# Windowed attention and a top-1 mixture of experts: 32-row products in batches of four slices, a fourth place for raw weights, and a last pass of 160 columns

## The chip, the cores and the metric

The kernel runs on one core of a Trainium2 chip. A core has a matrix engine (TensorE, "PE" in the profile; its weight loads are listed as "PEld"), three engines for elementwise work (VectorE "DVE", ScalarE "ACT", GpSimd "POOL"), and a queue engine (SyncE "SP") that here issues most of the DMA transfers. The metric is the device time of one execution in microseconds; lower is better. Three runs of the kernel before took 619.26 to 623.4 us, with a median of 622.6 us.

## The reference

The input of the first part is q, k and v of 8 batches, 8 heads, 576 positions and 64 features. Each position attends to itself and the 63 positions before it. The result is laid out as a matrix `x` of 4608 rows and 512 columns, and that goes through a mixture of experts in which each row uses one expert only:

```
logits = x @ w_gate                     # 4608 x 8
expert = argmax(logits);  gate = softmax(logits)[expert]
for e in range(8):
    xe = x[expert == e]
    out[expert == e] = gate * (max(xe @ w1[e], 0) @ w2[e])     # 512 -> 1024 -> 512
```

Everything is 32-bit floating point. With these inputs the eight experts get 669, 400, 748, 505, 592, 390, 566 and 738 rows.

## The kernel before, in words

**Stages.** The first 165 us or so compute the attention in 36 tiles of 128 rows, write the rows of `x` to a buffer in device memory (`xs`) and rank them by expert as they come. From then on the expert work goes in *passes*. A pass takes one expert and up to four blocks of 128 of its rows, gathers the rows from `xs` by an indirect DMA on POOL, and runs over the 1024 hidden features in eight *slices* of 128. The four early passes (experts 0 to 3, 256 rows each) start while the rest is still being ranked. Eleven late passes follow; their number of columns (rows of `x`) is fixed when the program is built, and which expert each one takes is worked out on the chip.

**Precision.** TensorE has a fast form of 32-bit products, fp32r, which keeps fewer bits of each operand. The kernel splits each operand into a high part (`whi`, `xh`, `hh`) and a remainder (`wlo`, `xl`, `hl`) and makes three fp32r products of them. A slice of a pass of `w` columns is then: twelve products of `w` columns for the first layer (lines 340 and 344: four pieces of 128 input features times three), the ReLU and its split (ACT `hh` on line 352, DVE `hl` on line 356), and three products of 512 columns for each block of rows in the second layer (line 312). The splits of the weights are ACT `whi` (line 253) and DVE `wlo` (line 250), 1024 columns per slice. In `expert`, the second layer of slice j is issued after the first layer of slice j+1, through `late` and `flush`.

**A last block that is not full.** Where the last block of a pass has 32 or 64 rows, `few` returns that number. Its second layer then uses plain 32-bit products of the raw weights (line 308): the 32 rows (`hf`, 128 features by 32) fill a quarter of TensorE's columns, and four products of 128 output columns each stand side by side in the four quarters (for 64 rows, two products of 256). Each plain 32-bit product appears as two MATMUL records.

**Passes.** `SLOTS` lists what late passes there are beside those of 256 columns: two of 416, two of 512, one of 320, one of 384. `plan` gives experts to these by their number of blocks and by how many rows their last block lacks; its small operations (8 numbers each) run on POOL (helpers on lines 719, 721 and 726) and on DVE, and DVE waits for POOL between them. What is left over goes to passes of 256 columns, five of them with these inputs (`ALWAYS`); more would run behind conditions at the end. `ORDER` is the order of the eleven: 256, 320, 416, 416, 512, 512, 384, and four times 256.

**Raw weights.** An expert's weights come in four transfers of 1 MB, two slices each, into three places of the pool `wr` that are used in turn. SP issues them (line 235) in program order, together with the transposing DMAs that lay out gathered rows for the next pass (`DMA_TRANSPOSE`, line 868, three or four ahead of a wide pass) and the read of the next expert's number (line 269). `ready`, called after each slice, prepares the next pass: it opens its weights after slice 3 and loads more of them after slices 4 and 6; the fourth load comes while the pass runs, from `split_`. For a pass that follows one with raw 32-bit products the loads come later (`held`), since the raw weights must stay until those products are done. In the first late pass the three transposing DMAs of the pass of 320 columns stand on SP ahead of the fourth load.

The functions that the change touches are `Weights`, `few`, `flush`, `expert`, `plan`, `ready` and `open_weights`.

## Time and profile before

| | |
|---|---|
| runs, us | 619.26, 622.6, 623.4 (median 622.6) |
| profiled execution, us | 618.67 |
| its span, us | 616.9 |
| PE busy | 583.2 us (95% of the span) |
| DVE, ACT, POOL busy | 377.8, 358.6, 211.9 us |
| late passes, roughly | 264 us to 609 us |

How to read it: PE's records overlap, since matmuls are pipelined, so a busy share near 100% means that one product follows the other, and the cost of a product is read from the distance between two starts, not from its duration. The chain of waits is followed back from the last instruction. In a timeline row the first number is the start and the second the length in us; square brackets give the idle time of the engine ahead of it and who ended it.

### The profile page before, as it was taken

How to read it: one execution, taken by the hardware profiler on the slowest of the kernel's cores; microseconds unless marked ns; L12 is line 12 of the kernel's file. 1: busy time of each engine (PE TensorE's matmuls, PEld its weight loads, DVE VectorE, ACT ScalarE, POOL GpSimd, SP SyncE). 2: the span in 40 equal slices, each digit the busy share in tenths (PEclk: the TensorE clock that was granted, in tenths of full speed). 3: DMA queues.
4: the chain of work that ended last, by engine and by line, in shares of the span. 5: the costliest groups of instructions: out<-in, count | busy, mean ns of one | idle time of the engine just before them, and what ended most of it. 6: DMA issues, size and time to landing. Idle time of an engine off the chain costs nothing.

```text
span 616.9 us, 16023 instructions
## 1 busy us (share of the span) xinstructions
PE 583.2 (95%) x6555; PEld 497.1 (81%) x6555; DVE 377.8 (61%) x680; ACT 358.6 (58%) x759; POOL 211.9 (34%) x212
## 2 busy tenths in 40 slices
PE   8899898887999999998999999999999999999995
PEld 4688787776977888997778888788888899999994
DVE  4677678886676996656555554454444535667651
ACT  4577677676435665658654646436426446667752
POOL 3656657667447125041315051050120311132011
PEclk9999999999899999999999999999999999999998
DMA  8978888963586676895939367393292473886731
GB/s 301 379 252 295 278 256 293 304 204 111 190 306 204 241 250 178 305 244 199 230 113 302 122 181 232 137 258 126 82 265 91 116 265 104 295 272 203 266 132 35
DMA packets 71748, 132.85 MB, mean 215 GB/s; under 512 B 42604, under 2 KB 43756, under 8 KB 64240
## 3 DMA queue, kind: packets, MB, share of 16 engines
q1 hardware_dynamic: 65392, 112.84, 56.8%
q0 software_dynamic: 6272, 18.88, 9.3%
q8 instruction: 53, 0.87, 0.6%
q14 instruction: 31, 0.25, 0.1%
HBM read 104.44 MB, written 19.40 MB: 201 GB/s over the span
## 4 chain that ended last, share of the span: by engine, by line
PE 65%; issue 12%; POOL 9%; DVE 6%; DMA 4%; ACT 2%; SPq 0%; POOLq 0%; DVEq 0%; ACTq 0%
PE e_b L340 19%; PE e_b L312 12%; PE e_b L344 9%; PE x_b L312 5%; PE t_b L312 4%; POOL pm L486 4%; PE m_b L312 4%; PE x_b L500 3%; PE s_b L443 2%; PE m_b L517 2%; DMA ring<-qkv 2%; DVE wlo L250 1%; DMA raw<-wall 1%; POOL out L294 1%; DMA xs<-xrow 1%
## 5 line engine op out<-in xcount | busy, mean ns | idle before, releaser
L250 DVE TENSOR_TENSOR wlo<-raw,whi 128x1024 fp32r<-128x1024 f32 (+1 forms) x126 | 147.9, 1174 | 55.8 <-ACT whi L253 55.0
L352 ACT ACTIVATE hh<-e_b 128x256 fp32r<-128x256 f32 (+2 forms) x120 | 52.3, 436 | 176.5 <-PE e_b L344 175.8
L294 POOL DMA_INDIRECT out<-ys,idx_sb x32 | 44.2, 1382 | 261.3 <-ACT ys L291 255.8
L253 ACT CAST whi<-raw 128x1024 fp32r<-128x1024 f32 (+1 forms) x121 | 121.5, 1005 | 3.5 <-DMA raw<-wall 3.4
L340 PE MATMUL e_b<-xh,whi 128*128 128x256 f32 (+4 forms) x352 | 110.8, 331 | 2.2 <-ACT whi L253 2.2
L356 DVE SCALAR_TENSOR_TENSOR hl<-e_b,hh 128x256 fp32r<-128x256 f32 (+2 forms) x120 | 58.1, 484 | 86.9 <-ACT hh L352 65.0
L486 POOL TENSOR_TENSOR pm<-tsb,cs 128x512 f32<-128x512 f32 x72 | 90.2, 1273 | 52.4 <-ACT tsb L479 46.3
L340 PE MATMUL e_b<-xl,whi 128*128 128x256 f32 (+4 forms) x352 | 107.9, 323 | 0.0
L340 PEld LDWEIGHTS e_b<-xh,whi 128*128 128x128 f32 x352 | 66.3, 188 | 14.2 <-ACT whi L253 4.4
L344 PE MATMUL e_b<-xh,wlo 128*128 128x256 f32 (+4 forms) x352 | 70.6, 322 | 0.1
L340 PEld LDWEIGHTS e_b<-xl,whi 128*128 128x128 f32 x352 | 66.4, 189 | 4.7
L470 ACT ACTIVATE pf<-s_b,mxs 128x64 f32<-128x64 f32 x288 | 63.2, 337 | 9.7 <-DVE mxs L462 7.1
L500 PE MATMUL x_b<-ring,pm 64*64 64x65 f32 x2176 | 47.7, 224 | 13.1 <-issue 6.8
L344 PEld LDWEIGHTS e_b<-xh,wlo 128*128 128x128 f32 x352 | 56.4, 188 | 3.4 <-DVE wlo L250 0.5
L500 PEld LDWEIGHTS x_b<-ring,pm 64*64 64x64 f32 x2176 | 41.9, 135 | 19.2 <-issue 12.5
L312 PE MATMUL e_b<-whi,hl 128*128 128x512 f32 x144 | 56.4, 392 | 0.7 <-DVE hl L356 0.7
L312 PE MATMUL e_b<-wlo,hh 128*128 128x512 f32 x144 | 56.5, 392 | 0.0
L312 PE MATMUL e_b<-whi,hh 128*128 128x512 f32 x144 | 56.5, 392 | 0.0
L872 ACT COPY joined<-halves 128x1024 uint16<-128x1024 uint16 x36 | 47.8, 1352 | 0.0
L191 POOL DMA_INDIRECT rows<-xs,idx_sb x32 | 37.6, 1174 | 26.9 <-issue 26.0
L524 ACT COPY xT<-m_b 128x512 f32<-128x512 f32 x36 | 21.1, 587 | 42.4 <-PE m_b L517 42.3
L443 PE MATMUL s_b<-ring 64*64 64x128 f32 x1024 | 41.4, 277 | 1.1 <-DMA ring<-qkv 0.6
(203 smaller groups left out, 1005.7 us busy)
## 6 DMA issues: line engine op xcount, KB each, us to landing
raw<-wall SPq DMA_DIRECT2D x58, 1024.0 KB
ring<-qkv SPq DMA_DIRECT2D x66, 386.0 KB
xs<-xrow SPq DMA_DIRECT2D x36, 256.0 KB
raw<-wall SPq DMA_DIRECT2D x8, 256.0 KB
rows<-xs SPq DMA_DIRECT2D x2, 1024.0 KB
ring<-qkv SPq DMA_DIRECT2D x4, 256.0 KB
halves<-planes SPq DMA_TRANSPOSE x36
ring<-qkv SPq DMA_DIRECT2D x4, 130.0 KB
```

Source lines behind the costliest of these rows:

```text
L250: nc.vector.tensor_tensor(out=lo[:, s], in0=raw[:, s], in1=hi[:, s], op=ALU.subtract)
L253: nc.scalar.copy(out=hi[:, s], in_=raw[:, s])
L294: ins = nc.gpsimd.indirect_dma_start(out=out, out_offset=bass.IndirectOffsetOnAxis(ap=ix, axis=0), in_=ys[0:n], in_offset=None, bounds_che ...
L312: nc.tensor.matmul(y[0:n], lhsT=x[:, us], rhs=ww[:, C:], start=(j == 0 and m == 0), stop=(j == NJ - 1 and m == 2))
L340: nc.tensor.matmul(hp[:, 0:w], lhsT=hi[:, ks], rhs=x[:, kk, 0:w], start=(kk == 0 and x is xh), stop=False)
L344: nc.tensor.matmul(hp[:, 0:w], lhsT=lo[:, kk * P:(kk + 1) * P], rhs=xh[:, kk, 0:w], start=False, stop=(kk == 3))
L352: nc.scalar.activation(out=hh[:, 0:r], in_=hp[:, 0:r], func=AF.Relu)
L356: nc.vector.scalar_tensor_tensor(out=hl[:, 0:r], in0=hp[:, 0:r], scalar=0.0, in1=hh[:, 0:r], op0=ALU.max, op1=ALU.subtract)
L443: nc.tensor.matmul(sp[cols, a, g], lhsT=q_r[rows, r, g], rhs=k_r[rows, r - 1:r + 1, g], start=True, stop=True)
L470: nc.scalar.activation(out=pf[:, g, a], in_=sp[:, a, g, 0], func=AF.Exp, bias=mx[:, h:h + 1], scale=SCALE)
L486: nc.gpsimd.tensor_tensor(out=pm[i], in0=t.rearrange("p (g q) -> p g q", g=NG), op=ALU.mult, in1=cc("mask")[:, i * P:(i + 1) * P].unsqueez ...
L500: nc.tensor.matmul(x_b[cols, a, g * V1:(g + 1) * V1], lhsT=pm[i][rows, g, cols], rhs=v_r[rows, c % RING - i, g], start=(i == 0), stop=(i = ...
```

## The change

The 64-row case of raw products goes away: `few` is true for 32 rows only, so the pass of 320 columns makes its last block with three fp32r products like any other. The 32-row products are collected over four slices (`some`, `BATCH`) and issued together, sixteen products in a row. The raw weights of slices 0 to 3 of such a pass must stay until then, so there is a fourth place for raw weights: `place`, which is the memory of two of the early passes' buffers of gathered rows (`xg[1]` and `xg[2]`, now one tile `xgs`). In late passes the second of the four transfers goes there, and the last load is issued after slice 0 of the running pass.

There is a new kind of pass, one of 160 columns: a full block and 32 rows. `plan` has a row for it (`p4`, `c4`), and one pass of 256 columns less is always there (`ALWAYS` 4). It is the last in `ORDER`. The experts 1 and 2 change places (`PERM`), on the host for the weights and the gate, so the four early passes still take the first four. The expert of 400 rows then needs two late blocks, the second with 16 rows, and it fits the new pass; four passes of 256 columns remain. Spacers (`SPACE`) and widths of small tables follow.

```diff
-SLOTS = ((4, 416, 2), (4, 512, 2), (3, 320, 1), (3, 384, 1))
+SLOTS = ((4, 416, 2), (4, 512, 2), (3, 320, 1), (3, 384, 1), (2, 160, 1))
+KINDS = len(SLOTS) + 1
+PERM = (0, 2, 1, 3, 4, 5, 6, 7)
...
-ALWAYS = 5
-TAIL = [5, 6, 8, 12, 18]
-ORDER = (6, 4, 0, 1, 2, 3, 5, 7, 8, 9, 10)
+ALWAYS = 4
+TAIL = [4, 5, 7, 11, 17]
+ORDER = (7, 4, 0, 1, 2, 3, 5, 8, 9, 10, 6)
...
+BATCH = 4
...
-    xg = [const.tile([P, 2, C], F32, name=f"xg{i}") for i in range(3)]
+    xgs = const.tile([P, 3, 2, C], F32, name="xgs")
+    xg = [xgs[:, i] for i in range(3)]
+    place = xgs[:, 1:3].rearrange("p i u c -> p i (u c)")
...
-            raw = self.raws[jj] = wr.tile([P, 2, 2 * C], F32, name="raw")
+            raw = place if self.late and jj == 1 else wr.tile([P, 2, 2 * C], F32, name="raw")
+            self.raws[jj] = raw
...
-            if self.far and not self.held and r and self.loaded < min(jj + 3, NJ // 2):
+            if self.far and r and self.loaded < min(jj + 3, NJ // 2):
                 self.load()
...
     def few(w):
 
-        n = w % P
-        return n if n in (LQ, W) else 0
+        return w % P == LQ
...
             if hf is not None and u + 1 == len(yp):
-                k = P // n
-                for g in range(k):
-                    nc.tensor.matmul(y[g * n:(g + 1) * n, 0:C // k], lhsT=hf[:, 0:n],
-                                     rhs=raw[:, C + g * C // k:C + (g + 1) * C // k], start=(j == 0), stop=(j == NJ - 1))
+                some.append((j, hf, raw))
+                if len(some) == BATCH:
+                    for i, x, ww in some:
+                        for g in range(QUAD):
+                            nc.tensor.matmul(y[g * LQ:(g + 1) * LQ, 0:P], lhsT=x, rhs=ww[:, C + g * P:C + (g + 1) * P],
+                                             start=(i == 0), stop=(i == NJ - 1))
+                    some.clear()
...
-            n = few(w)
-            r = w - n
+            r, hf = w, None
+            if few(w):
+                r, i = w - LQ, j % BATCH
+                hfs = hw.tile([P, BATCH, LQ], F32, name="hfs", bufs=2) if i == 0 else hfs
+                hf = hfs[:, i]
...
-            if wts.held and j % 2 == 0 and wts.loaded < j // 2 + 3:
+            if wts.late and j in (0, 2):
                 wts.load()
...
-        ev = of("ev2", two("ev", half, 2.0, ALU.is_ge), two("even", odd, 0.5, ALU.is_lt), ALU.mult)
-        of("ev3", ev, two("few", spare, float(P - LQ), ALU.is_ge), ALU.mult, want2[:, 0])
+        ev = of("ev2", two("even", odd, 0.5, ALU.is_lt), two("few", spare, float(P - LQ), ALU.is_ge), ALU.mult)
+        of("ev3", ev, two("ev", half, 2.0, ALU.is_ge), ALU.mult, want2[:, 0])
+        pair = of("pair", ev, two("one2", half, 1.0, ALU.is_ge), ALU.mult)
...
-        p3 = of("p3", odds, cm[:, 2], ALU.subtract)
+        of("p3", odds, cm[:, 2], ALU.subtract, more2[:, 0])
+        of("p4", pair, cm[:, 0], ALU.subtract, more2[:, 1])
...
         l1 = of("l3", two("third", cm[:, 3], -3.0, ALU.mult), l1, ALU.add)
+        l1 = of("l3b", two("pairs", cm[:, 4], -2.0, ALU.mult), l1, ALU.add)
...
-        wts[i] = Weights(expert_of(passes[i][0]), far=True, held=few(widths[i]) > 0)
+        wts[i] = Weights(expert_of(passes[i][0]), late=True)
...
+    order = list(PERM)
+    moe_w1, moe_w2, moe_w_gate = moe_w1[order], moe_w2[order], moe_w_gate[:, order]
```

Three places where the program's instructions move. The first is on PE, between two slices of a pass of 416 columns (`m_b`, `t_b` and the `e_b` of the second layer are accumulators of the four blocks; `xh` and `xl` belong to the first layer of the next slice). Before, each slice has this:

```order
L312 MATMUL t_b<-whi,hh 128x512
L312 MATMUL t_b<-wlo,hh 128x512
L312 MATMUL t_b<-whi,hl 128x512
L308 MATMUL m_b<-raw,hf 32x128 x4
L340 MATMUL e_b_3376<-xh,whi 128x416
L340 MATMUL e_b_3376<-xl,whi 128x416
```

Now, after the fourth slice and after the eighth, and nothing of the kind after the others:

```order
L324 MATMUL t_b<-whi,hh 128x512
L324 MATMUL t_b<-wlo,hh 128x512
L324 MATMUL t_b<-whi,hl 128x512
L319 MATMUL m_b<-raw,hfs 32x128 x8
L319 MATMUL m_b<-xgs,hfs 32x128 x8
L352 MATMUL e_b_3375<-xh,whi 128x416
L352 MATMUL e_b_3375<-xl,whi 128x416
```

Four groups of four products became one group of sixteen, half of it from the fourth place (`xgs`).

The second is on SP, from the third weight load of the first late pass on. Before:

```order
L235 DMA raw<-wall 128x2048
L868 DMA_TRANSPOSE halves<-planes 128x8x128 x3
L235 ISA
L235 DMA raw<-wall 128x2048
L269 TENSOR_LOAD es_sb
```

Now:

```order
L242 DMA raw<-wall 128x2048
L242 ISA
L242 DMA raw<-wall 128x2048
L888 DMA_TRANSPOSE halves<-planes 128x8x128 x3
L276 TENSOR_LOAD es_sb
```

The fourth load moved from behind the three transposing DMAs to ahead of them.

The third is on POOL, in `plan` (`want` is what DVE waits for next). Before:

```order
L719 TENSOR_SCALAR ev<-halfr 128x8
L719 TENSOR_SCALAR even<-odd 128x8
L726 TENSOR_TENSOR ev_3891<-ev,even 128x8
L719 TENSOR_SCALAR few<-spare 128x8
L726 TENSOR_TENSOR want_3842<-ev_3891,few 128x8
L719 TENSOR_SCALAR less<-spare 128x8
L726 TENSOR_TENSOR want_3842<-odds,less 128x8
L726 TENSOR_TENSOR p_3957<-odds,cm 128x8
```

Now:

```order
L733 TENSOR_SCALAR even<-odd 128x8
L733 TENSOR_SCALAR few<-spare 128x8
L740 TENSOR_TENSOR ev_3890<-even,few 128x8
L733 TENSOR_SCALAR ev<-halfr 128x8
L740 TENSOR_TENSOR want_3841<-ev_3890,ev 128x8
L733 TENSOR_SCALAR one_3895<-halfr 128x8
L740 TENSOR_TENSOR pair<-ev_3890,one_3895 128x8
L733 TENSOR_SCALAR less<-spare 128x8
L740 TENSOR_TENSOR want_3841<-odds,less 128x8
L740 TENSOR_TENSOR more_3960<-odds,cm 128x8
L740 TENSOR_TENSOR more_3960<-pair,cm 128x8
```

Two operations more stand ahead of the second `want`, one more right after it, and two (`pairs`, `l3b`) further down.

## Rows read from the trace of the kernel before

**Rows 1.** Page, parts 2 and 4: PE by slices of 15.4 us; the chain.
```profile
PE   8899898887999999998999999999999999999995
...
PE 65%; issue 12%; POOL 9%; DVE 6%; DMA 4%; ACT 2%; SPq 0%; POOLq 0%; DVEq 0%; ACTq 0%
```

**Rows 2.** Timeline of PE, one slice of the first pass of 416 columns.
```profile
325.96 0.39 PE L312 MATMUL t_b<-whi,hl 128*128 128x512 f32 x1
326.28 0.43 PE L308 MATMUL m_b<-raw,hf 128*32 128x128 f32 x8
326.64 0.46 PE L340 MATMUL e_b<-xh,whi 128*128 128x416 f32 x1
326.94 0.35 PE L340 MATMUL e_b<-xl,whi 128*128 128x416 f32 x1
327.13 0.35 PE L340 MATMUL e_b<-xh,whi 128*128 128x416 f32 x1
```

**Rows 3.** Timeline of PE in the attention stage: gate products and what follows.
```profile
64.81 1.08 PE L561 MATMUL m_b<-xT,wg_sb 128*32 128x128 f32 x32 [0.24 <-ACT xT L524]
65.83 1.10 PE L443 MATMUL s_b<-ring 64*64 64x128 f32 x32
```

**Rows 4.** Timeline of PE, one slice of the pass of 320 columns.
```profile
304.69 0.39 PE L312 MATMUL m_b<-whi,hl 128*128 128x512 f32 x1
305.00 0.65 PE L308 MATMUL x_b<-raw,hf 128*64 128x256 f32 x4
305.59 0.42 PE L340 MATMUL e_b<-xh,whi 128*128 128x320 f32 x1
```

**Rows 5.** Timeline of PE's weight loads, behind the raw products of rows 2.
```profile
326.64 0.19 PEld L340 LDWEIGHTS e_b<-xh,whi 128*128 128x128 f32 x1 [0.20 <-issue]
326.75 0.19 PEld L340 LDWEIGHTS e_b<-xl,whi 128*128 128x128 f32 x1
```

**Rows 6.** Timeline, the last slice of the last pass (256 columns) and the end.
```profile
605.07 0.28 PE L340 MATMUL e_b<-xh,whi 128*128 128x256 f32 x1
605.19 0.28 PE L340 MATMUL e_b<-xl,whi 128*128 128x256 f32 x1
...
606.50 0.39 PE L312 MATMUL e_b<-whi,hh 128*128 128x512 f32 x1
...
607.19 0.39 PE L312 MATMUL e_b<-whi,hh 128*128 128x512 f32 x1
...
608.75 1.37 ACT L291 ACTIVATE ys<-e_b,gate_sb 128x512 f32<-128x512 f32 x2 [1.67 <-PE e_b L312]
...
610.99 0.98 POOL L294 DMA_INDIRECT out<-ys,idx_sb  x1 [0.30 <-DVEq L1106]
```

**Rows 7.** Timeline of SP, ACT and PE in the first late pass.
```profile
264.10 5.85 SPq L868 DMA_TRANSPOSE halves<-planes  x3
...
278.40 1.04 ACT L253 CAST whi<-raw 128x1024 fp32r<-128x1024 f32 x1 [2.71 <-DMA raw<-wall]
...
279.50 0.39 PE L340 MATMUL e_b<-xh,whi 128*128 128x256 f32 x1 [1.43 <-ACT whi L253]
...
283.65 0.39 PE L340 MATMUL e_b<-xh,whi 128*128 128x256 f32 x1 [0.80 <-ACT whi L253]
```

**Rows 8.** Chain of waits in the same pass: the fourth load.
```profile
270.20 8.18 DMA raw<-wall
```

**Rows 9.** Timeline of POOL in `plan`.
```profile
191.20 0.23 POOL L719 TENSOR_SCALAR less<-spare 128x8 f32<-128x8 f32 x1
191.51 0.20 POOL L726 TENSOR_TENSOR want<-odds,less 128x8 f32<-128x8 f32 x1
...
193.88 1.07 POOL L726 TENSOR_TENSOR l<-four,left 128x8 f32<-128x8 f32 x1
```

**Rows 10.** Waits, 190 to 290 us: engine, for whom, us, times, longest.
```profile
DVE c02r L736 <- POOL want L726: 3.7, 1, 3.7
...
PE x_b L312 <- DVE hl L356: 1.1, 1, 1.1
```

More of the change, by code (lines that the diff above doesn't have):

```diff
@@ L72 @@
 AHEAD = 2
-SPACE = (159, 232)
+SPACE = (135, 48)
 SPLIT = 26
@@ L84 @@
                ("st0", E), ("eid", E), ("tcol", NT), ("row", P), ("first", 2 * EARLY), ("pcol", 1), ("scol", 1), ("ucol", 1),
-               ("kind", 5), ("at", 5)):
+               ("kind", KINDS), ("at", 5)):
     CO[_n] = (_off, _w)
@@ L105, in constants @@
     put("mask", np.concatenate([p % W <= q, p % W > q], 1))
-    put("desc", E - e)
+    put("desc", E - np.array(PERM)[None])
     put("ebase", REG * P * e)
@@ L122, in constants @@
     put("ucol", ucol[:, None])
-    is_ = kind[:, None] == np.arange(5)[None]
+    is_ = kind[:, None] == np.arange(KINDS)[None]
     put("kind", is_)
-    last = is_[:, 0] | is_[:, 2]
-    put("at", np.stack([last, -4 * is_[:, 0] - 3 * is_[:, 2], ~last, 3 * (is_[:, 1] | is_[:, 4]), 4 * is_[:, 4]], 1))
+    last = is_[:, 0] | is_[:, 2] | is_[:, 4]
+    put("at", np.stack([last, -4 * is_[:, 0] - 3 * is_[:, 2] - 2 * is_[:, 4], ~last, 3 * (is_[:, 1] | is_[:, 5]),
+                        4 * is_[:, 5]], 1))
     return c
@@ L178, in window_attention_then_top1_moe @@
     ones = const.tile([P, P], BF16, name="ones")
-    starts = const.tile([P, 5 * E], F32, name="starts")
+    starts = const.tile([P, KINDS * E], F32, name="starts")
     ones_f = const.tile([P, P], F32, name="ones_f")
@@ L209, in window_attention_then_top1_moe, with __init__ @@
     class Weights:
-        def __init__(self, ev, spread=0, far=False, held=False):
-            self.far, self.held = far, held
+        def __init__(self, ev, spread=0, far=False, late=False):
+            self.far, self.late = far, late
             self.ev, self.loaded, self.given, self.raws = ev, 0, 0, {}
@@ L269, in expert_of @@
         return nc.sync.value_load(es_sb[m:m + 1, 0:1], min_val=0, max_val=E - 1)
-    late = []
+    late, some = [], []
     def few(w):
-        n = w % P
-        return n if n in (LQ, W) else 0
+        return w % P == LQ
     def flush(final=False):
@@ L286, in finish @@
             ys = hw.tile([P, C], F32, name="ys", bufs=5)
-            k = P // n if hf is not None and u + 1 == len(yp) else 1
-            for g in range(k):
-                o, i = ys[0:n, g * C // k:(g + 1) * C // k], yp[u][g * n:(g + 1) * n, 0:C // k]
-                if g == 0:
-                    nc.scalar.activation(out=o, in_=i, func=AF.Copy, scale=gate)
-                else:
-                    nc.vector.tensor_scalar(out=o, in0=i, scalar1=gate, scalar2=None, op0=ALU.mult)
+            if hf is not None and u + 1 == len(yp):
+                for g in range(QUAD):
+                    o, i = ys[0:n, g * P:(g + 1) * P], yp[u][g * LQ:(g + 1) * LQ, 0:P]
+                    if g == 0:
+                        nc.scalar.activation(out=o, in_=i, func=AF.Copy, scale=gate)
+                    else:
+                        nc.vector.tensor_scalar(out=o, in0=i, scalar1=gate, scalar2=None, op0=ALU.mult)
+            else:
+                nc.scalar.activation(out=ys[0:n], in_=yp[u][0:n], func=AF.Copy, scale=gate)
             ins = nc.gpsimd.indirect_dma_start(
@@ L408, in window_attention_then_top1_moe @@
     nc.vector.memset(starts, 1.0)
-    for k in range(5):
+    for k in range(KINDS):
         nc.vector.memset(starts[:, k * E:k * E + 1], 0.0)
@@ L767, in plan @@
             yield
-        stt("c3", running("c3r", p3)[:, 0], float(SLOTS[3][2]), p3, ALU.is_le, ALU.mult, out=cm[:, 3])
+        ends = running("c34r", more2.rearrange("p k e -> p (k e)"), 2)
+        stt("c3", ends[:, 0], float(SLOTS[3][2]), more2[:, 0], ALU.is_le, ALU.mult, out=cm[:, 3])
+        stt("c4", ends[:, 1], float(SLOTS[4][2]), more2[:, 1], ALU.is_le, ALU.mult, out=cm[:, 4])
         yield
         l1 = of("l3", two("third", cm[:, 3], -3.0, ALU.mult), l1, ALU.add)
+        l1 = of("l3b", two("pairs", cm[:, 4], -2.0, ALU.mult), l1, ALU.add)
         p1 = two("p1", l1, 4.0, ALU.is_ge)
@@ L776, in plan @@
         l1 = of("l4", two("fourth", cm[:, 1], -4.0, ALU.mult), l1, ALU.add)
-        floor_of("ns", two("l5", l1, 0.0, ALU.max), 0.5, 0.25, cm[:, 4])
+        floor_of("ns", two("l5", l1, 0.0, ALU.max), 0.5, 0.25, cm[:, KINDS - 1])
         for _ in range(WAIT[3]):
             yield
-        sums = running("sums", cm.rearrange("p k e -> p (k e)"), 5)
-        nc.vector.tensor_copy(out=tot_sb, in_=sums[:, 4, E - 1:E])
+        sums = running("sums", cm.rearrange("p k e -> p (k e)"), KINDS)
+        nc.vector.tensor_copy(out=tot_sb, in_=sums[:, KINDS - 1, E - 1:E])
         yield
@@ L784, in plan @@
         kind, at = cc("kind"), cc("at")
-        mine = rt.tile([P, 5, E], F32, name="sums_", bufs=1)
-        nc.vector.tensor_tensor(out=mine, in0=sums, in1=kind.unsqueeze(2).to_broadcast([P, 5, E]), op=ALU.mult)
+        mine = rt.tile([P, KINDS, E], F32, name="sums_", bufs=1)
+        nc.vector.tensor_tensor(out=mine, in0=sums, in1=kind.unsqueeze(2).to_broadcast([P, KINDS, E]), op=ALU.mult)
         ends = small("ends")
@@ L899, in ready @@
         prepare(j, late_rows[i % 2], len(passes[i]), i, columns_of)
-        held = i > 0 and few(widths[i - 1]) > 0
+        held = i > 0 and few(widths[i - 1])
         if j == 3 + held:
```

10 lines of the change are left out of this document (5 added, 5 removed).

## The prediction, made before the changed kernel was run

> **What bounds the kernel now.** I read the page first. From the second half of the span on, PE's slices show 9 throughout, and of the chain that ended last 65% is PE [rows 1]. So in the late passes the time is the sum of PE's steps, and a step is the distance between the starts of two products. Then I read the timeline of PE for one slice of each kind of pass that the change touches [rows 2, 4, 6], to get these steps; then the places where PE had to wait: the first late pass, where a weight load came late [rows 7, 8], and the stretch around 190 us, where DVE waits for the small operations of `plan` on POOL and PE waits for DVE [rows 10].
>
> **32-row products in batches.** In a pass of 416 columns the last fast product of a slice is followed after 0.32 us, where its step is 0.23 [606.50 to 607.19 for three, rows 6]: 0.09 more. The raw products take 0.36 to the start of the next kind, and the first product of that kind takes 0.30 where the next takes 0.19: 0.11 more [rows 2]. Together 0.56 us per slice, 16 slices in the two passes: 9.0 us. The attention stage has exactly the new pattern: the gate's products, 32 records of 128 columns with 32 weight columns each, side by side in four quarters. From their start to the next kind it is 1.02 us [rows 3]. A batch then costs 0.09 + 1.02 + 0.11 = 1.22 us, and there are four: 4.9. The gain is **4.1 us**. If the batch did not overlap its four groups, it would take 4 x 0.36 + 0.20 = 1.64, and the gain would be 2.4; I take the row of the same pattern.
>
> **The pass of 320 columns.** Its raw products cost 0.31 - 0.23 = 0.08, then 0.59 [rows 4], then 0.11 as in rows 2: 0.78 us per slice. Three fast products of 512 columns take 0.69 [rows 6]. Over eight slices that is a gain of **0.7 us**. No fast product with 64 weight columns is in the trace; if changing to that width and back costs what it costs the raw ones, 0.19 per slice, it is a loss of 0.8. I take the gain, since the stream of columns is that of rows 6. `hh` and `hl` get a quarter longer there; ACT and DVE wait for PE in these passes, so this costs nothing as long as PE is the bound.
>
> **The last pass.** It has 160 columns where it had 256, and its second block makes raw products. The first layer has 12 products per slice with a step of 0.12 [605.07 to 605.19, rows 6]. What a step of 160 columns takes, no row shows. The steps at 512, 416 and 256 columns are 0.23, 0.19 and 0.12 [rows 2, 6], a line that gives 0.08 at 160. But each product has a weight load of 128 columns of its own, and where two loads stand back to back with nothing before them, the second starts 0.11 after the first [rows 5]. A step cannot then be shorter than the load, and I take 0.11: 8 x 12 x 0.01 = 1.0 us gained. The ends are 0.12 (nothing) and 0.08 (3.8 us).
> The Trainium skill says of weight loads the same (TensorE: Matmul & The Clock Gate, LDWEIGHTS): their time goes with the stationary operand's columns, about 107 ns for 128, whatever streams afterwards. This speaks against narrowing the pass, and by it the first layer would give next to nothing; the trace agrees, with its 0.11. The same page's section on the back-to-back gap gives an isolated product of 160 columns 69 ns, and the first layer would then give 4.9 us.
> The second layer loses the second block's three products. The end hangs on the moment when the first block of the last slice is done, at 608.75 [rows 6], so seven of the eight count: 7 x 0.69 = 4.8. Of the two batches the first counts, 1.22. The second runs after 608.75, and it has 2.24 us until the second scatter would start on POOL at 610.99 [rows 6], which it does not reach: free. Its cover is POOL's first scatter; without that, 1.2 us. Together this pass gives 1.0 + 4.8 - 1.2 = **4.6 us** (3.6 to 7.4).
>
> **The fourth place and the order of loads.** In the first late pass the three transposing DMAs hold SP from 264.10 for 5.85 us [rows 7], the fourth load starts at 270.20 and takes 8.18 us [rows 8], ACT waits 2.71 us for it, and PE loses 1.43 and, as ACT is then behind, 0.80 [rows 7]. In the new program this load stands ahead of the transposing DMAs, and the buffer that it takes was last read in the early pass before. Issued at 264.10 at the latest, even with 8.18 it lands at 272.3, ahead of 275.7, when ACT first asked (278.40 - 2.71). I take the whole 2.23: **2.2 us**. The ends are 0 (other transfers fill the room) and 2.7. What SP then issues behind it, the transposing DMAs, is asked for much later. In the other passes loads come a slice or two earlier than before, and PE waited for none; no gain.
>
> **The plan.** POOL gets five small operations more. One takes 0.23 or 0.20 and the next starts 0.31 later [rows 9], but 1.07 can also happen (193.88, while DVE ran a wide operation). Two stand ahead of `want`, for which DVE waits 3.7 us while `hl` is queued behind that wait and PE waits 1.1 us for `hl` [rows 10]: 0.6 us straight onto PE. The other three come ahead of later waits of the same chain, where PE's products still cover something; I count two thirds of their 0.9. Together **1.2 us lost** (0.5 to 2.5, if two of them take 1.07).
>
> The early passes read other experts' weights and rows, in the same numbers; DVE's scans of 48 instead of 40 numbers are below what can be told. These cost nothing.
>
> **Sum.** -4.1 - 0.7 - 4.6 - 2.2 + 1.2 = **-10.4 us**. The profiled execution took 618.67, so it would take 608.3. That one is faster than all three runs shown, whose median of 622.6 lies 3.9 above it; for the median of runs I say **612.2 us**. The bounds together, not all at one end, make 608.5 to 616.
>
> **Rivals.**
> *The fast product falls back below 256 columns.* Every fast product in the trace streams 256 columns or more; should a narrower one run like a plain 32-bit product, the last pass would be slower. A round of four plain ones, side by side, adds (1.02 - 0.36) / 3 = 0.22 us per 128 columns [rows 2, 3], 0.28 for 160. Then 96 products cost 96 x (0.28 - 0.12) = 15.4 more instead of 1.0 less, and the sum is +6.0: 628.6 us. It decides from a step of 0.22 on: (10.4 - 1.0) / 96 over 0.12. For it speaks only that nothing narrower was ever used here; against it, that the steps from 512 down to 256 lie on a line. 7%.
> *The columns alone decide.* Weight loads hide, the step is 0.08, the sum -13.2: 609.4 us. For it: at 256 columns loads and products overlap without a gap [rows 6]. Against it: 0.11 between two loads [rows 5]. This is what the gap formula quoted above would give. 13%.
> *The stall is moved, not removed, and the plan costs its worst.* The fourth load now shares its time with the transposing DMAs, and the loads of the next pass with the gathers; an 8.18 us landing [rows 8] shows how crowded it is. Then 2.2 is not gained and 1.3 more is lost: -6.9, 615.7 us. 16%.
> *The plan does not do what it says*, and a fifth pass of 256 columns runs behind the conditions: eight slices of 0.12 x 12 + 0.69 x 2 = 2.82 us [rows 6], 22.6 more: 634.8 us. The rows per expert speak against it: 400 rows are two early blocks and two late ones, the last with 16 rows. 2%.
> The forecast itself: 57%. 5% stay for what I have not seen.
>
> **The numbers.** The range takes in the forecast's own bounds, the second and third rival, and a microsecond or two for the spread of the runs, which is 4 us: 607.5 to 618. It leaves out the two slower cases, the unseen, and tails, about 2 in 10. A change under 1% (6.2 us) can't be told from none here; that is 616.4. Faster by more: nearly all of the forecast and of the second case, over half of the third, 0.77. Within 1%: 0.13. Slower: 0.10.
>
> **What would show it.** In the profile after, each pass of 416 columns has two groups of 32 records of about 1.0 us, and slices without one are 0.56 us shorter; the last pass has a step of 0.11 and a slice of about 2.0 us instead of 2.8; PE's two gaps in the first late pass are gone, and ACT's wait for the load with them; the gap of 1.1 around 191 us has grown to some 1.7. A step of 0.2 or more in the last pass, a DMA as the releaser of ACT's `whi`, or PE's busy share falling in the late passes would make it wrong.

## The result and the profile after

The changed kernel takes **610.41 us** (median; 610.16, 610.67, 609.82, 616.26) where the kernel before, its three runs shown ahead and one more of 618.6, takes 620.93. The ratio of the fast runs is 0.9858, 95% interval 0.981 to 0.9907 (that of the two medians is 0.983), so it is faster, by 1.4% or a little more. The forecast was 612.2 us and a change of -10.4. The profiled execution takes 610.16 us (span 608.4) against 618.67 (616.9): -8.5.

Two profiled executions can be compared only from the early passes on. Up to there the kernels of the ten runs below are nearly the same program, and yet the slice that starts at 159.74 us in the changed kernel's trace starts at 155.9 to 162.5 in theirs. From there on the granted clock is 1.00 both before and after (ahead of it 0.98 and 1.00), so the clock does not enter into the differences. The table goes by the starts of slices (the first product of a first layer), each stretch by its own length.

| stretch (us, before; after) | before | after | difference | forecast |
|---|---|---|---|---|
| start to a slice of the early passes (159.50; 159.74) | 159.50 | 159.74 | +0.2 | 0 |
| `plan` (to 211.78; 213.01) | 52.28 | 53.27 | +1.0 | +1.2 |
| rest of the early passes (to 261.00; 262.50) | 49.22 | 49.49 | +0.3 | 0 |
| first late pass (to 286.87; 285.76) | 25.87 | 23.26 | -2.6 | -2.2 |
| pass of 320, its last second layer included (to 321.78; 320.02) | 34.91 | 34.26 | -0.65 | -0.7 |
| passes of 416, likewise (to 400.37; 394.59) | 78.59 | 74.57 | -4.0 | -4.1 |
| 512, 384 and three of 256 (to 585.47; 579.70) | 185.10 | 185.11 | 0.0 | 0 |
| last pass to its first result copy (608.75; 599.07) | 23.28 | 19.37 | -3.9 | } |
| from there to the start of the last scatter (610.99; 602.64) | 2.24 | 3.57 | +1.3 | } -4.6 |
| end | 5.89 | 5.73 | -0.2 | 0 |

Four of the five terms of the forecast's sum hold to 0.4 us. The fifth, the last pass, gives 2.6 instead of 4.6.

The page answers to [rows 1]: PE by 40 slices, and the shares of the chain. PE stays the bound.
```profile
PE   8788889798898999999999999999999999999994
...
PE 74%; POOL 9%; DVE 6%; issue 6%; DMA 3%; ACT 2%; SPq 0%; POOLq 0%; DVEq 0%; ACTq 0%
```

The timeline of PE where a batch stands in a pass of 416 columns, and the next slice's start, answer to [rows 2]:
```profile
337.07 0.39 PE L324 MATMUL t_b<-whi,hl 128*128 128x512 f32 x1
337.39 0.64 PE L319 MATMUL m_b<-raw,hfs 128*32 128x128 f32 x16
337.85 0.62 PE L319 MATMUL m_b<-xgs,hfs 128*32 128x128 f32 x16
338.40 0.46 PE L352 MATMUL e_b<-xh,whi 128*128 128x416 f32 x1
338.69 0.35 PE L352 MATMUL e_b<-xl,whi 128*128 128x416 f32 x1
```
The batch is 32 records as in [rows 3], 16 from each of two buffers of weights (`xgs` is the new place): 0.32 from the last fast product, where its step is 0.23, then 1.01, then 0.29 where the next step takes 0.19 as in [rows 2]. That is 0.09 + 1.01 + 0.10 = 1.20 (forecast 1.22). Slices without a batch take 4.32 us, before 4.88.

The pass of 320 columns, beside [rows 4]: the third block's products now step at 0.23, like every other, with 64 weight columns and without a price at either end.
```profile
303.76 0.39 PE L324 MATMUL x_b<-wlo,hh 128*64 128x512 f32 x1
303.99 0.39 PE L324 MATMUL x_b<-whi,hl 128*64 128x512 f32 x1
304.21 0.31 PE L352 MATMUL e_b<-xh,whi 128*128 128x320 f32 x1
```

SP's queue and PE in the first late pass, beside [rows 7, 8]: the weight loads stand ahead of the transposing DMAs, and PE's two gaps of 1.43 and 0.80 have become one of 0.19. The two slices behind the late load, which took 4.39 and 4.15 us, take 2.80 and 3.15.
```profile
252.44 8.42 SPq L242 DMA_DIRECT2D raw<-wall  x2
265.60 5.65 SPq L888 DMA_TRANSPOSE halves<-planes  x3
...
282.56 0.38 PE L352 MATMUL e_b<-xh,whi 128*128 128x256 f32 x1 [0.19 <-ACT whi L260]
```

`plan`, beside [rows 9, 10]: DVE's wait for `want` and PE's for DVE now, then DVE's next wait in `plan`, before and now (engine, for whom; us, times, longest).
```profile
DVE c02r L750 <- POOL want L740: 4.1, 1, 4.1
...
PE x_b L324 <- DVE hl L370: 1.6, 1, 1.6
...
DVE c1r L736 <- POOL p L719: 1.8, 1, 1.8
...
DVE c1r L750 <- POOL p L733: 2.3, 1, 2.3
```
PE's wait for `hl` grew from 1.1 to 1.6, as the prediction had it for the two operations ahead of `want` (forecast 1.7). Two further stalls, 0.2 and 0.3 us in the slices at 206 and 209, come behind DVE's wait for `p`, which grew by 0.5: `pairs` and `l3b` stand ahead of it on POOL. DVE's own operations there, one of them new and some wider, took only hundredths more each.

The last pass, beside [rows 6]: a first layer, the start of its second layer, and the next slice.
```profile
594.12 0.23 PE L352 MATMUL e_b<-xh,whi 128*128 128x160 f32 x1
594.19 0.28 PE L352 MATMUL e_b<-xl,whi 128*128 128x160 f32 x1
594.30 0.28 PE L352 MATMUL e_b<-xh,whi 128*128 128x160 f32 x1
...
595.42 0.43 PE L324 MATMUL e_b<-whi,hh 128*128 128x512 f32 x1
595.68 0.39 PE L324 MATMUL e_b<-wlo,hh 128*128 128x512 f32 x1
...
596.15 0.24 PE L352 MATMUL e_b<-xh,whi 128*128 128x160 f32 x1
```
The step at 160 columns is 0.11, as forecast; the twelve products take 1.30 (594.12 to 595.42), before 1.43. The three of the second layer take 0.73 instead of 0.69, since the first step behind the narrow products is 0.26. The slice takes 2.03, 0.04 more than forecast.

And the end, PE, ACT, DVE and POOL in order of time:
```profile
598.97 1.08 PE L319 MATMUL e_b<-raw,hfs 128*32 128x128 f32 x32
599.07 0.69 ACT L302 ACTIVATE ys<-e_b,gate_sb 128x512 f32<-128x512 f32 x1 [1.06 <-PE e_b L324]
600.03 0.97 POOL L303 DMA_INDIRECT out<-ys,idx_sb  x1 [14.88 <-ACT ys L302]
600.12 0.36 ACT L298 ACTIVATE ys<-e_b,gate_sb 32x128 f32<-32x128 f32 x1 [0.35 <-PE e_b L319]
600.50 1.07 DVE L300 TENSOR_SCALAR ys<-e_b,gate_sb 32x128 f32<-32x128 f32 x3 [2.17 <-ACT ys L298]
602.64 0.88 POOL L303 DMA_INDIRECT out<-ys,idx_sb  x1 [1.63 <-issue]
```
Here is the loss. POOL's first scatter is over at 601.0, the second starts only at 602.64. Ahead of it stand, one behind the other: the batch (to 600.1), one copy on ACT, three on DVE that wait for ACT's (to 601.57), and 1.07 in which POOL waits for nothing that the profile shows.

A second, smaller loss is in the third slice of this pass, which takes 2.35 instead of 2.03. ACT makes two result copies of the pass before (581.93 and 582.63) ahead of `whi`; DVE's `wlo` follows late, and PE's next products begin at 585.56, 0.35 behind the one before:
```profile
582.63 0.69 ACT L302 ACTIVATE ys<-x_b,gate_sb 128x512 f32<-128x512 f32 x1
583.21 1.04 ACT L260 CAST whi<-xgs 128x1024 fp32r<-128x1024 f32 x1
...
584.28 1.22 DVE L257 TENSOR_TENSOR wlo<-xgs,whi 128x1024 fp32r<-128x1024 f32 x1 [2.39 <-ACT whi L260]
...
585.21 0.27 PE L352 MATMUL e_b<-xl,whi 128*128 128x160 f32 x1
585.56 0.68 PE L356 MATMUL e_b<-xh,wlo 128*128 128x160 f32 x4
```

### The profile page after: what moved, and what is told of

Same layout as the page of the kernel before. It is cut to its first block, busy times and chain, and to the rows that moved or that the text cites. A ratio compares the mean times of both kernels' runs of the same rounds, so it can differ in the third digit from the quotient of the medians.

```text
span 608.4 us, 16098 instructions
## 1 busy us (share of the span) xinstructions
PE 571.4 (94%) x6587; PEld 494.4 (81%) x6587; DVE 379.3 (62%) x684; ACT 357.3 (59%) x759; POOL 210.6 (35%) x217
## 3 DMA queue, kind: packets, MB, share of 16 engines
q0 software_dynamic: 6224, 18.88, 10.4%
## 4 chain that ended last, share of the span: by engine, by line
PE 74%; POOL 9%; DVE 6%; issue 6%; DMA 3%; ACT 2%; SPq 0%; POOLq 0%; DVEq 0%; ACTq 0%
PE e_b L352 21%; PE e_b L324 14%; PE e_b L356 11%; PE x_b L324 7%; POOL pm L500 5%; PE m_b L324 5%; PE t_b L324 5%; PE x_b L514 3%; PE s_b L457 2%; DMA ring<-qkv 2%; PE m_b L575 2%; PE m_b L531 2%; DVE wlo L257 1%; DMA xs<-xrow 1%; ACT xT L538 1%
## 5 line engine op out<-in xcount | busy, mean ns | idle before, releaser
L257 DVE TENSOR_TENSOR wlo<-raw,whi 128x1024 fp32r<-128x1024 f32 (+1 forms) x104 | 122.7, 1180 | 41.5 <-ACT whi L260 37.6
L367 ACT ACTIVATE hh<-e_b 128x256 fp32r<-128x256 f32 (+4 forms) x120 | 51.7, 431 | 164.4 <-PE e_b L356 157.8
L303 POOL DMA_INDIRECT out<-ys,idx_sb x32 | 40.7, 1270 | 253.6 <-ACT ys L302 242.7
L352 PE MATMUL e_b<-xh,whi 128*128 128x256 f32 (+5 forms) x352 | 107.8, 323 | 0.2 <-ACT whi L260 0.2
L352 PE MATMUL e_b<-xl,whi 128*128 128x256 f32 (+5 forms) x352 | 107.5, 322 | 0.0
L370 DVE SCALAR_TENSOR_TENSOR hl<-e_b,hh 128x256 fp32r<-128x256 f32 (+4 forms) x120 | 57.4, 478 | 75.8 <-ACT hh L367 57.6
L260 ACT CAST whi<-raw 128x1024 fp32r<-128x1024 f32 (+1 forms) x99 | 98.6, 997 | 1.2 <-DMA raw<-wall 1.2
L356 PE MATMUL e_b<-xh,wlo 128*128 128x256 f32 (+5 forms) x352 | 70.6, 322 | 0.1
L324 PE MATMUL e_b<-whi,hl 128*128 128x512 f32 x136 | 53.3, 392 | 0.7 <-DVE hl L370 0.7
L324 PE MATMUL e_b<-wlo,hh 128*128 128x512 f32 x136 | 53.4, 392 | 0.0
```

The source lines that it names most:

```text
L257: nc.vector.tensor_tensor(out=lo[:, s], in0=raw[:, s], in1=hi[:, s], op=ALU.subtract)
L260: nc.scalar.copy(out=hi[:, s], in_=raw[:, s])
L324: nc.tensor.matmul(y[0:n], lhsT=x[:, us], rhs=ww[:, C:], start=(j == 0 and m == 0), stop=(j == NJ - 1 and m == 2))
L352: nc.tensor.matmul(hp[:, 0:w], lhsT=hi[:, ks], rhs=x[:, kk, 0:w], start=(kk == 0 and x is xh), stop=False)
L356: nc.tensor.matmul(hp[:, 0:w], lhsT=lo[:, kk * P:(kk + 1) * P], rhs=xh[:, kk, 0:w], start=False, stop=(kk == 3))
L367: nc.scalar.activation(out=hh[:, 0:r], in_=hp[:, 0:r], func=AF.Relu)
```

## The experiments

Each is the changed kernel with the edit shown. Ratios are to the kernel before, run on the same chip in the same hour. Batches of one apart, their intervals overlap that of the changed kernel well (batches of two and the four widths have one run each and no ratio), so what an edit is worth is read from one trace of each kernel. Small waits between 213 and 262 us, up to 0.7 us in all, come and go from one execution to the next; "to the last scatter" is the time from the slice at 159.74 us to the start of the last scatter, 442.90 us in the changed kernel.

### Batches of one and of two

```diff
-BATCH = 4
+BATCH = 1
```


> The changed kernel with batches of one slice: each slice issues its own round of four 32-row products again, everything else stays. Theory (the gain lies in the batch: a round alone costs 0.56 us of PE's time, a batch of four 1.2): 16 x 0.56 - 4 x 1.2 = +4.1 us in the two passes of 416 columns, whose slices would all take about 4.9 us instead of 4.3 and 5.4 by turns. In the last pass seven rounds count instead of one batch, 7 x 0.56 - 1.2 = +2.7, and behind the last product of the first block one round of 0.36 stands instead of 1.08, -0.7. Together +6.1 us, 616.3 for a profiled execution against 610.16. Rival (the gain in these passes comes from something else that changed there, such as the loads that are issued earlier): +0 to +2 us, and the slices keep their 4.3.

Median 615.14 us, ratio 0.9936 (0.9907 to 0.9965). Two slices of a pass of 416 columns, PE:
```profile
333.57 0.46 PE L352 MATMUL e_b<-xh,whi 128*128 128x416 f32 x1
...
338.45 0.46 PE L352 MATMUL e_b<-xh,whi 128*128 128x416 f32 x1
```
To the last scatter 448.31: +5.4. In the two passes of 416 all slices but the first take 4.88, together +3.9; the changed kernel's own execution holds a stall of 0.2 there, so +4.1 is the price. In the last pass the slices take 2.59, that is 2.03 + 0.56. From the first result copy to the last scatter it takes 3.09 instead of 3.57, 0.5 less where 0.7 was expected: the round is over at 604.69, but ACT is still at the first block's copy and starts on the 32 rows at 604.95. Up to its first result copy the last pass loses 2.4 where 2.7 was expected, since the changed kernel's stall of 0.3 in the third slice does not show under slower slices. With the stall of 0.2, and 0.4 less of the small waits ahead of the late passes, this makes 5.4 of the 6.1. The gain of the passes of 416 is the batch's, and the rival is out.

```diff
-BATCH = 4
+BATCH = 2
```


> The changed kernel with batches of two slices. A round alone costs 0.56 us of PE's time and a batch of four 1.2. Theory (rounds follow each other at about 0.21 once the first has begun, whatever their number; what a batch saves is the start and the two changes between kinds of product): 0.77 for two, 8 x 0.77 - 4 x 1.2 = +1.4 us in the passes of 416 columns. Rival (only four rounds together keep the four quarters busy; two cost 0.2 + 2 x 0.36 = 0.92): +2.6 us there.

One run, 610.76 us. The timeline of PE around a batch:
```profile
327.09 0.39 PE L324 MATMUL t_b<-whi,hl 128*128 128x512 f32 x1
327.41 0.64 PE L319 MATMUL m_b<-raw,hfs 128*32 128x128 f32 x16
327.98 0.45 PE L352 MATMUL e_b<-xh,whi 128*128 128x416 f32 x1
```
0.57 from the first raw product to the next kind, where one round takes 0.36 [rows 2] and four take 1.01: each further round adds 0.21. A slice with a batch and the one behind it take 4.99 + 4.41, so a batch of two costs 9.40 - 2 x 4.32 = 0.76 (expected 0.77). The two passes take 1.1 us more, 1.3 without the stall of 0.2 (expected 1.4). What a batch saves is the start and the changes of kind; two rounds overlap as well as four.

### The wide last pass and the old plan back

```diff
-SLOTS = ((4, 416, 2), (4, 512, 2), (3, 320, 1), (3, 384, 1), (2, 160, 1))
+SLOTS = ((4, 416, 2), (4, 512, 2), (3, 320, 1), (3, 384, 1))
-PERM = (0, 2, 1, 3, 4, 5, 6, 7)
+PERM = tuple(range(8))
-ORDER = (7, 4, 0, 1, 2, 3, 5, 8, 9, 10, 6)
+ORDER = (6, 4, 0, 1, 2, 3, 5, 7, 8, 9, 10)
...
```
`ALWAYS`, `TAIL`, the constants and `plan` go back with them.

> The changed kernel with the passes and the plan of the kernel before: no pass of 160 columns, a last pass of 256, the experts in their own order; batches, the fourth place and the fast products of the pass of 320 columns stay. Theory A (the terms as forecast: last pass 4.6 us gained, plan 1.2 lost): +3.4 us against the changed kernel. Theory B (as the two traces read: the last pass gained 2.7 us, because the second batch and the copies behind it lengthen the end by 1.2 and there is a stall of 0.3, and the plan lost 1.3): +1.4 us, with the time from the first result copy of the last slice to the end 1.2 us shorter than in the changed kernel and the slices around 190 us back at the times of the kernel before. Rival C (the order of the experts itself costs or gains something): the early passes would differ by more than 0.2 us.

Median 610.32 us, ratio 0.9871 (0.9835 to 0.9907): no difference from the changed kernel that runs can tell. PE's wait in `plan` and the last scatter, right behind the one before it, are those of the kernel before:
```profile
195.58 0.50 PE L323 MATMUL x_b<-whi,hl 128*128 128x512 f32 x1 [1.09 <-DVE hl L369]
...
605.50 0.97 POOL L302 DMA_INDIRECT out<-ys,idx_sb  x1 [0.30 <-DVEq L1119]
```
The old plan takes 1.0 less (25.15 instead of 26.16 from the slice at 186.85 to that at 213.01), and the last pass to its last scatter 25.30 instead of 22.94. The early passes agree to 0.3 us otherwise; rival C's mark of 0.2 can't be told from chance, since the stretch behind `plan` takes 49.49 and 49.71 in two executions of the changed kernel itself, and 49.27 here. So theory B stands in its terms: the narrow pass brings 2.4 to 2.6 and its plan takes 1.0 of it back. But to the last scatter this kernel takes 443.02, only +0.1, and not the +1.4 that B expected: its late slices of 256 columns take 2.77 us where they take 2.80 in the kernels before and after, which with the pass of 320 comes to 0.8; the changed kernel's stall of 0.2 in the passes of 416 and 0.2 in the early passes are the rest. No theory foresaw that; see the shifted columns below.

### The fourth load behind the transposing DMAs

```diff
-            if wts.late and j in (0, 2):
+            if wts.late and j in ((2,) if wts.opening else (0, 2)):
...
+        wts[i].opening = i == 0
```


> The changed kernel, in the first late pass only with the fourth weight load issued behind the three transposing DMAs instead of ahead of them; its buffer stays as free as it was. Theory (the order of SP's queue is what removed the stall): ACT waits about 2.7 us for this load again, PE's slices there take 4.4 and 4.15 us again, +2.2 to +2.6 us at the end. Rival (the additional place is what matters, since the load can start without waiting for a buffer): the load starts when the transposing DMAs have been issued, lands in 2 to 3 us, and nothing is lost, 0 to +0.5 us.

Median 611.82 us, ratio 0.9902 (0.9872 to 0.9932). SP's queue, the chain's piece for the load, ACT's wait (us, times, longest) and PE's gaps:
```profile
267.26 6.02 SPq L888 DMA_TRANSPOSE halves<-planes  x3
...
273.53 7.49 DMA raw<-wall
...
ACT whi L260 <- DMA raw<-wall: 2.3, 1, 2.3
...
282.14 0.38 PE L352 MATMUL e_b<-xh,whi 128*128 128x256 f32 x1 [0.92 <-ACT whi L260]
286.31 0.39 PE L352 MATMUL e_b<-xh,whi 128*128 128x256 f32 x1 [0.78 <-ACT whi L260]
```
Both gaps are back, the first smaller than in the kernel before (0.92 instead of 1.43), and the pass takes 2.1 us longer, just under what the theory expected. The load waits for no buffer here and still takes 7.5 us, where the rival had 2 to 3. That is not long for such a load: of the eleven `raw` loads that are issued between 224 and 290 us in this trace the median lands after 8.2 us. What costs is that it is issued at 273.53, where in the changed kernel it has been issued by 260.86 (252.44 + 8.42). The order of SP's queue removed the stall; the place alone would not have. Whether the order without the place would have done it was not tried.

### Four widths in the last pass

```diff
+            v = (256, 160, 128, 64)[j // 2] if w == 160 else w
...
-                    nc.tensor.matmul(hp[:, 0:w], lhsT=hi[:, ks], rhs=x[:, kk, 0:w], ...
+                    v_ = max(v, w) if kk == 0 else v
+                    nc.tensor.matmul(hp[:, 0:v_], lhsT=hi[:, ks], rhs=x[:, kk, 0:v_], ...
```
The products with `lo` take `v` columns too.

> The changed kernel with the first layer of its last pass at four widths: in slices 0 and 1 the fast products stream 256 columns, in 2 and 3 the 160 of the changed kernel, in 4 and 5 128, in 6 and 7 64 (the first two of each slice never under 160). The results of the last pass lack the columns left out. Theory (a step cannot be shorter than the load of the product's own 128 weight columns): 0.12 at 256, then 0.11 at 160, at 128 and at 64 alike; the slices of 64 columns take the same 2.0 us as those of 160. Rival 1 (the columns decide and the changed kernel's 0.11 is only the price of 160): 0.08 or less at 128 and about 0.05 at 64, slices of 64 at least 0.5 us shorter. Rival 2 (fast products under 256 columns pay something of their own): the step grows as the width falls.

One run, 611.2 us. The first layer at 128 and at 64 columns, and the next slice:
```profile
590.03 0.27 PE L354 MATMUL e_b<-xl,whi 128*128 128x128 f32 x1
590.14 0.28 PE L354 MATMUL e_b<-xh,whi 128*128 128x128 f32 x1
...
594.81 0.24 PE L354 MATMUL e_b<-xh,whi 128*128 128x160 f32 x1
...
595.39 0.28 PE L354 MATMUL e_b<-xh,whi 128*128 128x64 f32 x1
595.50 0.28 PE L354 MATMUL e_b<-xl,whi 128*128 128x64 f32 x1
...
596.83 0.24 PE L354 MATMUL e_b<-xh,whi 128*128 128x160 f32 x1
```
The step is 0.12 at 256 columns and 0.11 at 160, at 128 and at 64; the slice with 64 takes 2.02 (594.81 to 596.83), that with 160 takes 2.03. From somewhere under 256 on the columns no longer matter, and both rivals are out: nothing falls back, and nothing is gained by fewer columns. That it is the load which sets the 0.11 rests on [rows 5]; no run changed the weight columns of a narrow fp32r product. Nor is 0.11 a bound for every product with 128 weight columns: the bf16 products on line 681 of the changed kernel, each with such a load of its own, step at 0.07 at 160 columns and at 0.025 at 20.
The Trainium skill (TensorE: Matmul & The Clock Gate, Back-to-back issue gap) gives about 81 ns for pairs of a weight load and a product of 128 columns, and names no type. This trace disagrees for fp32r: 0.11 us at 128 and at 64 alike. For the load by itself the Trainium skill (TensorE: Matmul & The Clock Gate, LDWEIGHTS) has a formula that makes about 107 ns of 128 columns, an estimate. The 0.11 is close to it.

### The last copies all on ACT

```diff
-                    if g == 0:
+                    if g == 0 or final:
```


> The changed kernel with all four copies of the very last 32 rows on ACT, where before one was on ACT and three followed on DVE. Theory (the last scatter waits for two engines; the second of these waits is an instruction of its own on POOL, and the scatter starts 1.03 us behind it, where the first scatter starts 0.27 us behind its copy): the four copies take 4 x 0.36 us and end at the same time as now, but the scatter starts 0.3 us behind them, -0.8 us at the end. Rival 1 (a scatter of these rows needs 1 us from its last copy whoever makes it): 0 +- 0.1 us. Rival 2 (POOL is still busy with the first scatter): 0, too, and the start of the second scatter stays 1.6 us behind the end of the first.

Median 609.01 us, ratio 0.9857 (0.9825 to 0.9889).
```profile
601.30 1.48 ACT L298 ACTIVATE ys<-e_b,gate_sb 32x128 f32<-32x128 f32 x4 [0.35 <-PE e_b L319]
...
603.37 0.88 POOL L303 DMA_INDIRECT out<-ys,idx_sb  x1 [1.17 <-ACT ys L298]
```
The copies end at 602.78, and the scatter starts 0.59 behind them, not 1.07 and not the expected 0.3. From the first result copy to the last scatter it takes 3.11 instead of 3.57: -0.46. So who makes the last copy does matter, by half of what the theory said; the other 0.3 stays open. Both rivals expected 0. Against the second speak the traces with batches of one and of two, too: there POOL's first scatter is over 1.17 and 1.20 us ahead of the second, in the changed kernel 1.63, and the second starts 1.07 behind DVE's last copy in all three.

### `pair` behind `want2`

```diff
-        odds = of("odds", two("one", half, 1.0, ALU.is_ge), odd, ALU.mult)
+        one = two("one", half, 1.0, ALU.is_ge)
+        odds = of("odds", one, odd, ALU.mult)
...
-        pair = of("pair", ev, two("one2", half, 1.0, ALU.is_ge), ALU.mult)
         of("p2", odds, two("less", spare, float(W), ALU.is_ge), ALU.mult, want2[:, 1])
+        pair = of("pair", ev, one, ALU.mult)
```


> The changed kernel with the small operations that it put ahead of want taken out of the way: one2 repeats one and is dropped, pair stands behind want2 in POOL's order. Theory (each of the small operations ahead of DVE's scan goes straight onto PE): the slice at 189 us that takes 4.67 in the changed kernel takes 4.2 again, -0.5 us; the two stalls at 206 and 209 (0.2 and 0.3 us), which hang on the operations behind c3 and c4, stay. Rival 1 (the wider scans and the later operations set the chain): 0 to -0.1. Rival 2 (POOL catches up later, the stalls at 206 and 209 go too, being the same delay carried on): -1.0 us.

Median 610.8 us, ratio 0.9892 (0.9814 to 0.9969).
```profile
189.00 0.50 PE L324 MATMUL x_b<-whi,hl 128*128 128x512 f32 x1 [1.09 <-DVE hl L370]
```
DVE's wait for `want` is 3.7 us again and PE's 1.09. The slice takes 4.18 again, -0.49, and the stalls of 0.2 and 0.3 in the fifth and sixth slice behind it stay: the theory, and neither rival. But to the last scatter it takes 444.47, **+1.6**. From the first late pass on most slices are slower by 0.03 or 0.04: 4.36 instead of 4.32 in the passes of 416, 5.57 instead of 5.54, and 2.84 and 2.80 by turns where all were 2.80; those of 320 and 160 columns are not. Dropping `one2` had taken two small arrays out of the memory ahead of the columns, which so start 64 bytes earlier.

### The columns shifted by 32 bytes

```diff
-SPACE = (135, 48)
+SPACE = (135, 56)
```


> The changed kernel with eight numbers more in the unused room ahead of the late passes' columns, so that these start 32 bytes further on; nothing else moves. In the kernel with the wide last pass all late slices of 256 columns took 2.77 us, in the kernels before and after 2.80, and there the distance of the columns' first byte from that of the weights was 64 modulo 128, here 32. Theory (where the columns lie against the weights sets a small part of the step): 2.77 here too, 24 slices x 0.03 and some tenths in the other passes, -0.7 to -1.2 us. Rival (the 0.03 is of that execution, such as the granted clock): 2.80, no difference.

Median 609.77 us, ratio 0.9867 (0.9795 to 0.9939). Two slices of 256 columns, PE:
```profile
525.96 0.28 PE L352 MATMUL e_b<-xh,whi 128*128 128x256 f32 x1
...
528.73 0.28 PE L352 MATMUL e_b<-xh,whi 128*128 128x256 f32 x1
```
2.77 us, in all late slices of that width, and 3.81 instead of 3.83 at 320. With the columns 32, 64 and 96 bytes (modulo 128) from the weights the slice takes 2.80, 2.77 and 2.82 on the average, in seven, three and one of the programs here. The theory holds. The distance goes with the time, not the columns' own place: by the addresses in the built programs, the columns start at 96 modulo 128 in the kernel with the wide last pass (weights at 32) and in that of `pair` (weights at 0), and the slices take 2.77 and 2.82. To the last scatter it takes 442.76, only 0.1 less: 0.8 us went into a stall at 363 us, in the second pass of 416 columns, that this execution has and most have not (DVE's `wlo`, behind copies that lay out the next pass's rows; the run with four widths lost 2.5 us at the same place, of which the trace puts 1.9 to PE's own issue). What decides on that stall was not tried.

### All of it, and the changed kernel once more

> The changed kernel as it is, for comparison beside the next kernel. By the runs so far its median here should lie 7 to 10 us under that of the kernel before. In its trace the start of the last scatter should again come 3.57 us behind the start of the first result copy of the last slice, and the third slice of the last pass should again take 2.35 us.

Median 608.97 us, ratio 0.9883 (0.9832 to 0.9933). That is 9.3 under the median of the kernel before (618.25). The tail is 3.57 again and the third slice of the last pass 2.34; to the last scatter 442.92, without the stall of 0.2 but with more of the small waits.

The second kernel has the edits of the last copies and of `pair`, `SPACE = (135, 72)`, and:
```diff
+            elif share and u == 1:
+                nc.vector.tensor_scalar(out=ys[0:n], in0=yp[u][0:n], scalar1=gate, scalar2=None, op0=ALU.mult)
             else:
                 nc.scalar.activation(out=ys[0:n], in_=yp[u][0:n], func=AF.Copy, scale=gate)
...
+            if i == MANY - 1:
+                share.append(i)
...
```


> The changed kernel with four small edits: the last copies all on ACT (measured -0.46 us up to the last scatter), pair behind want2 and one2 dropped (-0.49), the columns' start where they lie 64 modulo 128 from the weights (-0.7; the room ahead of them is set anew for that, since the dropped number array moved them), and, new, the second of the two result copies of the pass before the last on DVE instead of ACT. Theory for the new one (in the last pass ACT makes these two copies of 0.69 ahead of whi, so wlo comes late and PE waits 0.3 us): the slice of 2.35 us takes 2.03, -0.3 us. Together -2.0 us from the slice at 159.7 us, behind which the executions of one program agree, to the last scatter. Rival for the new one (wlo is late because DVE itself is): DVE gets a copy more, nothing is gained. Rival for all (gains in single places are lost again at the next wait): under 1 us in all. The medians of runs differ by 2 us or so between chips and hours, so against the kernel beside it -2 us should just be seen.

Median **607.94 us**, ratio 0.9824 (0.9783 to 0.9865). DVE's copy and `wlo` in the last pass, and the last scatter:
```profile
581.76 0.75 DVE L302 TENSOR_SCALAR ys<-x_b,gate_sb 128x512 f32<-128x512 f32 x1 [0.72 <-PE x_b L326]
582.73 1.22 DVE L257 TENSOR_TENSOR wlo<-xgs,whi 128x1024 fp32r<-128x1024 f32 x1 [0.23 <-ACT whi L260]
...
601.01 0.88 POOL L305 DMA_INDIRECT out<-ys,idx_sb  x1 [1.18 <-DVEq L1133]
```
The third slice takes 2.03, -0.3: ACT's two copies were what made it late. To the last scatter it takes 440.22, **-2.7** against the changed kernel beside it. Of this 0.46 lie in `plan`, 0.8 in the slices of 256 and 320, 0.3 and 0.46 in the last pass, and 0.5 in the small waits between 245 and 262 us that come and go. Without these it is 2.2, near the 2.0 expected, and the rival for all is out. By the medians it is 1.0 us faster; the two intervals overlap, so the runs alone don't show it. One trace of each does, place by place.

## Why the prediction was right, and where it was wrong

**Batches.** Right, with its reason: 1.20 per batch against 1.22 from the gate's products, and the cost grows by 0.21 per round.

**The pass of 320.** Right. The 64 weight columns cost nothing at either end here, so the prediction's bound of a loss of 0.8 does not apply to this kind of product.

**The fourth load.** Right in cause, 0.4 too low in size: it added up PE's two gaps, and a gap is counted from the end of the record before it, which lasts 0.39 where its step is 0.23, so it shows 0.16 too little. Behind the first gap PE also waited 0.2 for `wlo`. The two slices were 2.9 too long in all (4.39 and 4.15 against 2.80), and 0.35 of that is left. With the order undone 2.1 come back. The third rival (the stall is only moved) did not happen in this pass.

**The plan.** +1.0 against +1.2: 0.5 for the two operations ahead of `want` and 0.5 for the three later ones, of which the prediction had let two thirds count. Taking the first two away gives the 0.5 back.

**The last pass.** The sum was 4.6 and it gave 2.6. The step at 160 columns was right (0.11), so the second rival fell by what [rows 5] show. **The step that failed** is this: "The second runs after 608.75, and it has 2.24 us until the second scatter would start on POOL at 610.99 [rows 6], which it does not reach: free." The batch indeed ended in time, 1.0 us behind the first block's last product. What the step left out is all that stands between a block's last product and its scatter: a full block has one copy, this one four, one behind the other on two engines, and then POOL's start. Together they take 1.1 (the batch) + 1.4 (the copies) + 1.1 (POOL) = 3.6 from the first result copy, where the cover is 2.24. The loss is 3.57 - 2.24 = 1.3. The prediction had a price for the case ("Its cover is POOL's first scatter; without that, 1.2 us"); that it lies so near is luck, for it was the batch's time alone. A batch shorter by three rounds gives 0.5 of the loss back and copies on one engine 0.5 as well, each tried by itself, so no single one of the three is the cause.
Another 0.3 went to ACT's two copies, which the prediction did not look at: narrower slices leave ACT 2.0 us where it had 2.8. The remaining 0.3 is the step of 0.26 behind narrow products, eight times 0.04.

**The time.** 612.2 was set 3.9 above the forecast's own execution, as the kernel before had stood to its median. Here execution and median fell together (610.16 and 610.41). The 2 us too many in the last pass and the 3.9 worked against each other, and the result lies well inside the range for the wrong reason as well as the right ones. That the medians differ by 10.5, as the forecast change of 10.4 has it, is luck, too: the executions differ by 8.5.

## What to carry to other kernels

A block that leaves PE sooner is not yet out of the kernel: count its copies and its store up to the last instruction, and put the block with the most steps behind its products anywhere but at the end (not tried here; a last pass with two full blocks has the shorter end, 2.24). In these traces a fast product's step follows its columns down to 0.12 at 256 and stays at 0.11, the distance of two weight loads, at 160 and below; there fewer columns buy nothing, while whole products saved still do. A gap that the profile shows can be shorter than the delay: compare starts. Before believing a gain of 1 us, compare stretch by stretch between the same two slices; and when arrays are added or dropped, look whether slices far away changed by some hundredths.

## What the runs showed of the hardware that was not expected

- Where the moving operand starts in memory against the weights goes with up to 1% of a slice's time: 2.77 us at a distance of 64 bytes modulo 128, 2.80 at 32, 2.82 on the average at 96; in the passes of 416 columns it is 4.32, 4.32 and 4.36, in those of 512 5.54, 5.54 and 5.57. Why was not found out; the value at 96 bytes rests on one program.
- At the end of the last pass an indirect scatter starts 0.27 us behind the single copy that it waits for (the first one), 0.59 behind the last of four copies on ACT, and 1.07 behind the last of three on DVE (the second one, in two kernels). Why was not found out.
- A fast 32-bit product (fp32r) with its own 128 weight columns has the same step, 0.11 us, at 160, 128 and 64 columns, at a granted clock of 1.00 in that stretch, the upper of the two levels. For 160 the prediction had it from [rows 5].
